# Longer contiguous runs for the r, k, v and expert-weight loads of an attention-then-experts kernel

## The chip, the cores and the metric

One core of one Trainium2 chip. The metric is device time in microseconds (us); lower is better. Times of one kernel are given as the median of its runs. Where two kernels are compared, a ratio is given too: the mean time of one kernel's fast runs over the mean of the other's fast runs from the same rounds on the same chip, with a 95% interval. It is therefore not quite the ratio of the medians. A run counts as slow when it took over 1.5% more than the fastest of its kernel.

A trace covers one execution. In it PE is TensorE's matmuls, PEld its weight loads, DVE is VectorE, ACT is ScalarE, POOL is GpSimd, SP is SyncE; a letter q after an engine's name means its sequencer, which issues DMAs. "L390" is line 390 of the kernel that the trace belongs to.

## The reference

A decayed linear attention, then a layer of experts that picks one expert for each whole sequence.

```python
B, H, S, D = 4, 8, 768, 48                 # r, k, v: [B, H, S, D] float32
state = zeros(B, H, D, D)
for t in range(S):
    kt, vt, rt = k[:, :, t], v[:, :, t], r[:, :, t]
    cur = einsum('bhd,bhe->bhde', u[None] * kt, vt)
    y[:, :, t] = einsum('bhd,bhde->bhe', rt, state + cur)
    state = w[None, :, :, None] * state + einsum('bhd,bhe->bhde', kt, vt)

x = y.transpose(0, 2, 1, 3).reshape(B, S, 384)
logits = x.mean(axis=1) @ w_gate           # [B, 8]
e = argmax(logits, axis=1)                 # one expert for a whole sequence
for b in range(B):                         # w1: [8, 384, 1024], w2: [8, 1024, 384]
    out[b] = softmax(logits)[b, e[b]] * (relu(x[b] @ w1[e[b]]) @ w2[e[b]])
```

The expert of a sequence is known only after its last row, so the weights of sequence b are loaded, and its matmuls done, while the attention of sequence b+1 runs. The last sequence's expert is a tail on its own.

## The kernel before

The attention goes in 24 chunks n of 128 rows (six per sequence). A chunk's k, r and v come by three DMAs, eight chunks ahead. A row of one head is 48 floats, so these loads move runs of 192 bytes.

```python
    AHEAD = 8
    inp = ctx.enter_context(tc.tile_pool(name="inp", bufs=AHEAD + 1))
    opool = ctx.enter_context(tc.tile_pool(name="opool", bufs=4))
    # ... (cut)
    def load(n):
        # ... (cut)
        for name, src in (("k32", k), ("r32", r), ("v32", v)):
            t = inp.tile([128, H, D], FP32, tag=name, name=f"{name}_{n}")
            nc.sync.dma_start(out=t, in_=src[b, :, s0 : s0 + C, :].transpose([1, 0, 2]))
```

GpSimd multiplies k and r by powers of the decay, TensorE transposes both (eight transposes into one PSUM tile), and ScalarE copies the eight results out in one instruction, `tw`. VectorE then forms `prod` for the bonus term, masks the scores (`gt`), adds up the chunk's output (`xn`) and masks the running state (`st`).

```python
    def prep(n):
        # ... (cut)
        nc.gpsimd.tensor_mul(kp[i][:, :, 0:D], k32, dk[:, m])
        nc.gpsimd.tensor_mul(rp[i][:, :, 0:D], r32, dr[:, m])
        vb = work.tile([128, H, D], BF16, tag="vb", name=f"vb{n}")
        nc.gpsimd.tensor_copy(vb, v32)

    def transposes(n):
        twp = pp_tw.tile([128, 2 * NP, 128], BF16, tag="tw", name=f"twp{n}")   # one PSUM buffer
        for o, src in ((NP, kp[i]), (0, rp[i])):
            for p in range(NP):
                nc.tensor.transpose(out=twp[:, o + p, :], in_=..., identity=ident)
        tw = work.tile([128, 2 * NP, 128], BF16, tag="tw", name=f"tw{n}")
        nc.scalar.copy(tw, twp)
```

The expert's weights come by two DMAs on GpSimd's queue, which also turn float32 into bf16. A partition gets three runs of `w1` and eight of `w2`. Each 128-row output tile `ob` is scaled by VectorE or ScalarE and stored by the sync queue, the same queue that issues the loads, in program order.

```python
        w1 = wpool.tile([128, NCT, F], BF16, tag="w1", name=f"w1_{b}")
        nc.gpsimd.dma_start(
            out=w1, in_=moe_w1[ds(ev, 1)].rearrange("o (ct p) f -> p (o ct) f", p=128))
        # ... w2 likewise, "o (ft p) m -> p (o ft) m" (cut)
    def mm1(b, w1, ht, ft, sb):        # hp: relu(x @ w1), 3 matmuls per tile
        #   lhsT=w1[:, ct, 128 * ft : 128 * ft + 128]
    def mm2(b, w2, ht, gw, si, half, cell):
        # ... (cut)
            ob = opool.tile([128, DM], FP32, tag="ob", name=f"ob{b}_{si}")
            # scaled by ACT for odd si, by DVE for even si
            nc.sync.dma_start(out=out[b, 128 * si : 128 * si + 128, :], in_=ob)

    for n in range(N):
        # ... (cut)
        if n + AHEAD < N:
            load(n + AHEAD)
        if n + 2 < N:
            prep(n + 2)
        if b and ci == 0:
            weights(b - 1)
        # transposes(n+1), up to five expert jobs, outputs(n), state(n), scores(n+1) ...
```

There are four buffers for `ob` and six output tiles per sequence.

## Time and profile before

| | before |
|---|---|
| time, median of 3 | 173.91 us (173.81 to 174.37) |
| span of the traced execution | 172.5 us |
| TensorE matmuls busy | 131.3 us, 76% |
| DMA packets | 85,217, of which 73,728 of 192 bytes |
| first `prod` / last expert's first `hp` / end | 13.8 / 149.7 / 172.5 us |

The table of 40 slices (each slice is 4.3 us; a digit is a share in tenths, 9 meaning 90% or more; PEclk is the granted TensorE clock):

```profile
PE   0035788768879998997007999899999979299991
PEclk9999999999999999999555899999999999969998
DMA  3989998999999989999999930059920018990042
```

Up to slice 11 TensorE is not full while the DMA engines are. From slice 12 TensorE is the limit, with one hole (slices 19 and 20, 82 to 91 us), during and after which the clock is granted by half.

The first batch has nothing but attention. The chain of waits, followed back from the end of the program, alternates there between small steps of VectorE and of TensorE (columns: start, duration, what):

```profile
21.14 0.55 DVE xn L255
21.69 0.47 DVE st L281
22.16 0.88 DVE prod L208
...
23.35 0.87 PE twp L196 x8
24.23 0.32 PE y L245 x4
24.55 0.33 PE y L250 x8
```

One round is one chunk: the next `xn` starts at 24.97, 3.84 us later.

The hole has a name in the waits (what waited, for what: us in total, times, longest):

```profile
DVE ob L390 <- DMA out_dram<-ob: 12.4, 1, 12.4
```

VectorE waited 12.4 us for the store of an earlier output tile, because all four `ob` buffers were full. The sync queue's timeline says why the store was late (start, duration, then the DMA issued):

```profile
71.78 5.45 SPq L81 DMA_DIRECT2D k<-in_k_dram  x1
77.32 4.21 SPq L81 DMA_DIRECT2D r<-in_r_dram  x1
...
86.15 0.69 SPq L81 DMA_DIRECT2D v<-in_v_dram  x1
86.93 1.27 SPq L391 DMA_DIRECT2D out_dram<-ob  x2
```

The first `ob` was begun at 71.9 us. Its store is issued at 86.93, when the queue has got through the loads that stand before it in the program.

Two groups of instructions that the change touches (after the bar: busy us in all, mean ns of one, then idle before it and for whom), and the DMA lines (packets; share of the 16 engines' time; issues with KB each and median us to landing):

```profile
L202 ACT COPY tw<-twp 128x1024 bf16<-128x1024 bf16 x24 | 24.3, 1011 | 17.9 <-PE twp L196 17.8
L365 PEld LDWEIGHTS <-w 128*128 128x128 bf16 x192 | 17.4, 103 | 15.5 <-issue 5.9
```

```profile
DMA packets 85217, 25.81 MB, mean 150 GB/s; under 512 B 76240, under 2 KB 83664, under 8 KB 85200
...
q1 hardware_dynamic: 79440, 19.29, 60.2%
q0 software_dynamic: 5760, 6.29, 22.6%
...
w<-in_moe_w_dram POOLq DMA_DIRECT2D x8, 768.0 KB, 10.9
```

q1 carries the loads and stores of the sync queue, q0 the weights.

### The profile page before, as it was taken

To read this page: it belongs to the slowest core of one execution; us is meant where nothing else is said; L and a number is where in the kernel's file an instruction comes from. 1 tells how busy PE (TensorE), PEld (TensorE's weight loads), DVE (VectorE), ACT (ScalarE), POOL (GpSimd) and SP (SyncE) were. 2 spreads that over 40 slices of the span, in tenths; PEclk is the share of its full clock that TensorE was granted. 3 is DMA by queue.
4 is the path that set the end of the run, shared out by engine and by line. 5 is a ranking of instruction groups with operands and counts; after the bars stand their busy time and mean duration, and the time that the engine had idled before them with its cause. 6 is when DMAs were issued, how large, how long until landed. Compare 5 with 4: busy or idle time off the path is not lost.

```text
span 172.5 us, 3663 instructions
## 1 busy us (share of the span) xinstructions
PE 131.3 (76%) x1392; PEld 88.9 (52%) x1392; DVE 91.5 (53%) x227; ACT 73.5 (43%) x121; POOL 87.8 (51%) x114
## 2 busy tenths in 40 slices
PE   0035788768879998997007999899999979299991
PEld 0024667657666665665004666566666454144550
DVE  3045888885785776860007567687677432022220
ACT  2929433432434674343002667334666422135221
POOL 4384788888987677667002577775661112000000
PEclk9999999999999999999555899999999999969998
DMA  3989998999999989999999930059920018990042
GB/s 88 188 153 197 187 188 166 194 179 197 177 192 198 192 164 206 174 194 185 185 243 256 256 52 6 0 91 224 245 88 0 0 49 155 226 212 0 1 174 102
DMA packets 85217, 25.81 MB, mean 150 GB/s; under 512 B 76240, under 2 KB 83664, under 8 KB 85200
## 3 DMA queue, kind: packets, MB, share of 16 engines
q1 hardware_dynamic: 79440, 19.29, 60.2%
q0 software_dynamic: 5760, 6.29, 22.6%
q8 instruction: 11, 0.18, 0.5%
q14 instruction: 6, 0.05, 0.1%
HBM read 27.15 MB, written 4.72 MB: 185 GB/s over the span
## 4 chain that ended last, share of the span: by engine, by line
PE 48%; DVE 18%; DMA 12%; issue 5%; SPq 5%; POOL 4%; ACT 4%; POOLq 0%; DVEq 0%; ACTq 0%
PE hp L365 16%; PE op L381 13%; PE twp L196 7%; SPq L81 5%; DVE prod L208 5%; DMA w<-in_moe_w_dram 5%; DVE xn L255 3%; DVE ht L374 3%; DMA ubc<-in_u_dram 3%; DMA v<-in_v_dram 2%; DVE st L281 2%; PE y L250 2%; PE y L245 2%; DMA out_dram<-ob 2%; PE xp L297 2%
## 5 line engine op out<-in xcount | busy, mean ns | idle before, releaser
L365 PE MATMUL hp<-xt,w 128*128 128x384 bf16 x192 | 42.8, 348 | 4.1 <-DMA w<-in_moe_w_dram 3.4
L236 POOL TENSOR_TENSOR vt<-vb,tcol 128x384 bf16<-128x384 bf16 x24 | 19.9, 830 | 42.6 <-DVE tcol L233 42.6
L381 PE MATMUL op<-w,ht 128*128 128x384 bf16 x192 | 35.4, 329 | 0.2 <-DVE ht L374 0.2
L202 ACT COPY tw<-twp 128x1024 bf16<-128x1024 bf16 x24 | 24.3, 1011 | 17.9 <-PE twp L196 17.8
L372 ACT ACTIVATE ht<-hp 128x384 bf16<-128x384 f32 x44 | 21.6, 492 | 20.3 <-PE hp L365 19.8
L184 POOL TENSOR_TENSOR kp<-k,dk 128x384 bf16<-128x384 f32 x24 | 23.9, 997 | 4.2 <-ACT dk L128 4.2
L365 PEld LDWEIGHTS <-w 128*128 128x128 bf16 x192 | 17.4, 103 | 15.5 <-issue 5.9
L185 POOL TENSOR_TENSOR rp<-r,dr 128x384 bf16<-128x384 f32 x24 | 24.4, 1019 | 0.0
L306 ACT COPY xt<-xp 128x384 bf16<-128x384 bf16 x24 | 11.5, 479 | 29.0 <-PE xp L297 27.7
L381 PEld LDWEIGHTS <-ht 128*128 128x128 bf16 x192 | 17.7, 99 | 10.2 <-issue 0.6
L255 DVE TENSOR_TENSOR xn<-vt,y 128x384 bf16<-128x384 bf16 x24 | 13.2, 551 | 16.2 <-PE y L250 15.2
L390 DVE TENSOR_SCALAR ob<-op,gw 128x384 f32<-128x384 f32 x12 | 7.4, 616 | 24.2 <-DMA out_dram<-ob 12.4
L374 DVE TENSOR_SCALAR ht<-hp 128x384 bf16<-128x384 f32 x20 | 11.0, 552 | 16.9 <-PE hp L365 16.6
L297 PE MATMUL xp<-ident,xn 128*128 128x128 bf16 x72 | 9.8, 257 | 10.9 <-DVE xn L255 10.9
L220 DVE TENSOR_TENSOR gt<-at,maskT 128x512 bf16<-128x512 f32 x24 | 16.4, 682 | 0.6 <-PE at L212 0.6
L234 DVE TENSOR_TENSOR gt<-at,maskT 128x512 bf16<-128x512 f32 x24 | 16.2, 677 | 0.0
L208 DVE TENSOR_TENSOR prod<-tw 128x512 bf16<-128x512 bf16 x24 | 14.2, 590 | 2.2 <-ACT tw L202 2.2
L212 PE MATMUL at<-tw 48*128 48x128 bf16 x192 | 11.6, 254 | 3.9 <-ACT tw L202 3.5
L187 POOL CAST vb<-v 128x384 bf16<-128x384 f32 x24 | 13.8, 575 | 0.0
L388 ACT ACTIVATE ob<-op,gw 128x384 f32<-128x384 f32 x12 | 7.0, 582 | 15.6 <-PE op L381 14.5
L196 PE MATMUL twp<-ident,kp 128*128 128x128 bf16 x96 | 11.7, 261 | 1.5 <-DVE U L160 1.5
L196 PE MATMUL twp<-ident,rp 128*128 128x128 bf16 x96 | 12.2, 266 | 0.0
(65 smaller groups left out, 153.3 us busy)
## 6 DMA issues: line engine op xcount, KB each, us to landing
w<-in_moe_w_dram POOLq DMA_DIRECT2D x8, 768.0 KB, 10.9
k<-in_k_dram SPq DMA_DIRECT2D x24, 192.0 KB, 4.5
r<-in_r_dram SPq DMA_DIRECT2D x24, 192.0 KB, 4.6
v<-in_v_dram SPq DMA_DIRECT2D x24, 192.0 KB, 4.6
out_dram<-ob SPq DMA_DIRECT2D x24, 192.0 KB, 3.4
wbc<-in_w_dram SPq DMA_DIRECT2D x1, 192.0 KB, 3.6
ubc<-in_u_dram SPq DMA_DIRECT2D x1, 192.0 KB, 4.4
wT<-in_w_dram SPq DMA_DIRECT2D x2, 0.8 KB, 2.8
```

The source lines that it names most:

```text
L184: nc.gpsimd.tensor_mul(kp[i][:, :, 0:D], k32, dk[:, m])
L185: nc.gpsimd.tensor_mul(rp[i][:, :, 0:D], r32, dr[:, m])
L196: nc.tensor.transpose(out=twp[:, o + p, :], in_=src[:, 2 * p : 2 * p + 2, :].rearrange("s a b -> s (a b)"), identity=ident,)
L202: nc.scalar.copy(tw, twp)
L208: nc.vector.tensor_mul(prod, tw[:, 0:NP, :], tw[:, NP : 2 * NP, :])
L220: nc.vector.tensor_mul(gt[:, 0], at[0], maskT)
L234: nc.vector.tensor_mul(gts[n][:, 1], at[1], maskT)
L236: nc.gpsimd.tensor_mul(vt, vbs[n], tcol.to_broadcast([128, H, D]))
L255: nc.vector.tensor_add(xn, vts[n].rearrange("s h d -> s (h d)"), yp[:, 0:DM])
L365: nc.tensor.matmul(out=hp[:, 0:SB], lhsT=w1[:, ct, 128 * ft : 128 * ft + 128], rhs=xts[b][:, ct, SB * sb : SB * sb + SB], start=(ct == 0), ...
L372: nc.scalar.activation(out=o, in_=hp[:, 0:SB], func=ACT.Relu)
L381: nc.tensor.matmul(out=op[:, 0:DM], lhsT=ht[:, ft, 128 * si : 128 * si + 128], rhs=w2[:, ft, :], start=(ft == 0), stop=(ft == NFT - 1),)
```

## The change

The intent is fewer, longer packets:

- **r** comes in eight groups of three chunks. Partition p of a group holds rows 3p, 3p+1, 3p+2, one run of 576 bytes per head. The columns of the transposed r then come interleaved, so the copy out of PSUM writes every third column and a chunk reads its 128 columns as one piece. A whole group must be transposed before its first chunk can start.
- **k and v** of sequences 1 to 3 come by one DMA per tensor and sequence, into a tile that keeps 16 unused columns after each row of 48.
- **Weights**: the rows of `w1` and `w2` are dealt out so that each partition's share is one run; `hp` reads its weights with a stride of eight columns to make up for it, and the output of the attention is transposed with a stride of three.
- To keep engines even, `vb` goes from GpSimd to ScalarE in the first two sequences, and `st` from VectorE to ScalarE in the first. The first three products of r are done by VectorE.
- In the program, all loads now precede the first store.

The diff, cut to its core:

```diff
-    AHEAD = 8
-    inp = ctx.enter_context(tc.tile_pool(name="inp", bufs=AHEAD + 1))
+    inp = ctx.enter_context(tc.tile_pool(name="inp", bufs=NCH))
+    binp = ctx.enter_context(tc.tile_pool(name="binp", bufs=2))
+    rinp = ctx.enter_context(tc.tile_pool(name="rinp", bufs=3))
+    rtp = ctx.enter_context(tc.tile_pool(name="rtp", bufs=3))
+    def load_batch(b):
+        for name, src in (("k32", k), ("v32", v)):
+            t = binp.tile([128, H, NCH, DP], FP32, tag=name + "b", name=f"{name}b_{b}")
+            nc.sync.dma_start(
+                out=t.rearrange("p h c d -> p (h c) d")[:, :, 0:D],
+                in_=src[b].rearrange("h (c p) d -> p (h c) d", p=128),
+            )
+    def load_r(g):
+        b, gi = divmod(g, NCH // GRP)
+        t = rinp.tile([128, H, GRP, D], FP32, tag="r32", name=f"r32_{g}")
+        nc.sync.dma_start(
+            out=t.rearrange("p h c d -> p h (c d)"),
+            in_=r[b, :, GRP * C * gi : GRP * C * (gi + 1), :].rearrange(
+                "h (p c) d -> p h (c d)", c=GRP),
+        )
     # ... (cut: issue order of the first loads, constants, the rest of prep)
-        nc.gpsimd.tensor_copy(vb, v32)
+        if n < 2 * NCH:
+            nc.scalar.copy(vb, raw.pop(("v32", n)))
+        else:
+            nc.gpsimd.tensor_copy(vb, raw.pop(("v32", n)))
+    def prep_r(j):
+        g, c = divmod(j, GRP)
+        eng = nc.vector if g == 0 else nc.gpsimd
+        eng.tensor_mul(rp[j % NR][:, :, 0:D], rraw[g][:, :, c, :], dr[:, c])
     # ... (cut: eight transposes as before, of k's chunk n and of r's chunk n + 3)
-        nc.scalar.copy(tw, twp)
+        if j < N:
+            g, c = divmod(j, GRP)
+            if c == 0:
+                rts[g] = rtp.tile([128, NP, C, GRP], BF16, tag="rt", name=f"rt{g}")
+            nc.scalar.copy(rts[g][:, :, :, c], twp[:, NP : 2 * NP, :])
+        if n >= 0:
+            kt = work.tile([128, NP, 128], BF16, tag="kt", name=f"kt{n}")
+            nc.scalar.copy(kt, twp[:, 0:NP, :])
     # ... (cut)
-            out=w1, in_=moe_w1[ds(ev, 1)].rearrange("o (ct p) f -> p (o ct) f", p=128))
+            out=w1.rearrange("p ct f -> p (ct f)"), in_=moe_w1[ds(ev, 1)].rearrange("o (p ct) f -> p (o ct f)", ct=NCT))
     # ... (cut: w2 likewise)
-                out=hp[:, 0:SB], lhsT=w1[:, ct, 128 * ft : 128 * ft + 128],
+                out=hp[:, 0:SB], lhsT=w1[:, ct, ft::NFT],
     # ... (cut)
+    for j in range(GRP):
+        prep_r(j)
     late_constants()
-    transposes(0)
+    for j in range(GRP):
+        transposes(0 if j == 0 else -1, j)
     # ... in the loop over n:
-        if n + AHEAD < N:
-            load(n + AHEAD)
+        if ci == 0 and 1 <= b and b + 1 < B:
+            load_batch(b + 1)
+        if n % GRP == 0 and n // GRP + 3 < NG:
+            load_r(n // GRP + 3)
```

## The prediction

> **What bounds the kernel now** (timeline, 40-slice table, waits):
>
> 1. 0 to 50 us: one chunk per 3.84 us (xn starts at 21.1, 25.0, 28.8, 32.7). The chain goes round DVE prod 0.88, PE bonus 0.27, eight transposes 0.87, output groups 0.65, DVE xn 0.5, DVE st 0.47. POOL (3.4 us per chunk) and the DMA engines (90% busy) run just under it.
> 2. 50 to 138 us: TensorE, 0.9 busy, 4.5 to 5 us per chunk, with one hole from 80.6 to 91.6 us. The waits name it: DVE's ob waits 12.4 us for the output store. All four ob buffers are full because the first store issues at 86.9 us: the sync queue is in order and still pushing loads (0.9 to 5.5 us per issue instead of 0.4[...]). The granted clock is 0.5 from 82.8 to 96.4 us (six hp in 1.94 us, later 1.15).
> 3. The tail: 8.0 us of waiting for the last w1, then matmuls.
>
> Loads are bound by packets: 73,728 of 192 B, median 15 ns each per engine, about 1.0 us per 1,024; 1,536 B take 66 ns. The Trainium skill ("DMA: Bandwidth & Descriptors", Specifications) asks for 512 B or more for line rate; the trace agrees (12.8 against 23 B/ns).
>
> **What the change does**
>
> - r: 24 loads of 192 B runs become 8 of 576 B. Estimated from those two sizes at 29 ns a packet: 24 us of DMA become 15. k and v keep 49,152 packets of 192 B, in fewer DMAs: 48 us, unchanged.
> - Weights: 1,408 packets per expert (9.7 us) become a few hundred long ones; I expect 8.5 to 9 us, 0.7 off the tail.
> - All loads now precede the stores and depend only on buffers, so they run ahead. DMA work up to the last load sums to 84 us, against 101; the first store should issue near 80 us, when ob4 is nearly wanted. The stall shrinks from 10.6 us to 0 to 3, and the half clock goes too: the skill ("TensorE: Matmul & The Clock Gate", Part 1) puts it after an idle window of about 3.4 us.
> - First batch: st goes to ACT, vb leaves POOL: 0.47 us off the chain, 3.35 per chunk.
> - Added before the first score: three rp products on DVE (0.6 each), three transposes with copies one after another in one PSUM buffer, ubc behind a larger r load: first prod at 18 instead of 13.8 us. tw (1.01) becomes two ACT copies of about 0.59. The first batched v load, 6,144 packets, may land 0 to 4 us late for chunk 6.
> - Strided weight loads for hp should hide behind 164 ns matmuls.
>
> **Sum:** start +4.5, first-batch chain -2.5, late v +2, stall -9, clock -2.5, tail -0.7, fewer conflicts -0.7: 165 us, range 159 to 171. Faster by over 2%: 0.82; within 2%: 0.14; slower: 0.04.
>
> **Right if** ob's wait for the store falls below 4 us, the half clock after 80 us vanishes, packets drop below 69,000, the first xn starts near 22 us, chunks of batch 0 are 3.35 us apart. **A step is wrong if** r packets take well over 29 ns, or hp exceeds 164 ns each.
>
> **What would make it wrong:** large k and v DMAs block the sync queue as long as before, so the stall stays (171); chunk 6 waits longer; strided weight loads or ACT copies slow the TensorE stage; or the start costs less (160).

## More of the kernel before

The four groups of experiments ran on three chips, at different times, and the kernel before took 173.9 to 176.3 us in them (medians), so kernels of different groups are compared by their ratios to the kernel before.

The clock's row prints 9 also where the trace has no record, and before 55.5 us it has none. What the clock was there shows in the spacing of the transposes: one every 107 ns up to 55 us, as in the recorded half clock at 95 us, and one every 56 ns from there on. So the first 55 us ran at half the clock.

## The result, and the profile after

| | before | after |
|---|---|---|
| time, median | 173.86 us of 4 (173.80 to 174.37) | 185.62 us of 4 (183.73 to 186.89) |
| ratio of fast runs | | 1.0588 (95%: 1.053 to 1.0647) |
| span of the traced execution | 172.5 us | 185.1 us |
| TensorE matmuls busy | 131.3 us, 76% | 135.1 us, 73% |
| DMA packets | 85,217 | 35,585 |

The change made the kernel slower by about 6%. Two of the four runs after count as slow; the ratio leaves them out. The trace after spans 185.1 us (the record gives 182.8 for the profiled run). That is at the long end of the four timed executions, whose spans were 181.8 to 185.0 us, and would count as slow by the same rule, so the differences between the two traces add up to 12.6 us where the ratio says about 10. The steps on which the argument rests come back in fast runs: the late start in a_now and a_ob6, the first hole in a_now, the second in b_w.

The 40 slices after (4.6 us each):

```profile
PE   0013558865678799899809999899399989299990
PEclk9999999999999999999995899999969999969999
DMA  3889999989999999999962000099410016980042
```

TensorE starts later, and there are now two holes: slice 20 (93 to 97 us) is the old one, and slice 28 (130 to 134 us) is new. After each the clock falls.

The waits after:

```profile
DVE ob L444 <- DMA out_dram<-ob: 8.8, 2, 7.2
...
DVE prod L255 <- ACT rt L242: 6.0, 1, 6.0
...
ACT ob L442 <- DMA out_dram<-ob: 3.3, 1, 3.3
...
ACT vb L218 <- DMA v32b<-in_v_dram: 2.9, 1, 2.9
```

The first line is the wait that should have gone: 7.2 us of it remain from the first hole, and 1.6 with the 3.3 of ScalarE's line are the second. The other two lines are the new start and the first batched v.

The sync queue's timeline, and the three DMAs in the chain of waits that answer to it (start, duration):

```profile
23.30 7.34 SPq L90 DMA_DIRECT2D v32b<-in_v_dram  x1
...
66.05 9.19 SPq L90 DMA_DIRECT2D v32b<-in_v_dram  x1
75.34 7.27 SPq L100 DMA_DIRECT2D r<-in_r_dram  x1
83.54 7.25 SPq L445 DMA_DIRECT2D out_dram<-ob  x3
```

```profile
23.30 17.99 DMA v32b<-in_v_dram
...
83.54 12.52 DMA out_dram<-ob
...
122.24 10.96 DMA out_dram<-ob
```

The first store is indeed asked for earlier, at 83.54 instead of 86.93, but takes 12.5 us to land instead of 3.4, because the loads asked for just before it are still in the engines (counted below, under the step that failed). A store at 122.24, which has no counterpart in the old chain, takes 11 us.

The start, in ScalarE's timeline (the bracket says how long the engine was idle before, and what released it):

```profile
15.83 1.01 ACT L242 COPY rt<-twp 128x512 bf16<-128x512 bf16 x1 [5.21 <-PE twp L233]
...
17.93 1.01 ACT L242 COPY rt<-twp-1_1_238 128x512 bf16<-128x512 bf16 x1 [0.67 <-PE twp-1_1_238 L233]
19.62 1.01 ACT L242 COPY rt<-twp-1_2_244 128x512 bf16<-128x512 bf16 x1 [0.67 <-PE twp-1_2_244 L233]
```

The three copies of the first r group go one after another through the single PSUM buffer, each of the first two followed by the next four transposes. The first `prod` starts at 20.66, against 13.76.

The groups and DMA lines that answer to those of before:

```profile
L419 PEld LDWEIGHTS <-w 128*128 128x128 bf16 x192 | 25.3, 151 | 15.0 <-issue 7.6
...
L242 ACT COPY rt<-twp 128x512 bf16<-128x512 bf16 x22 | 22.5, 1024 | 11.6 <-PE twp L233 11.2
...
L245 ACT COPY kt<-twp 128x512 bf16<-128x512 bf16 x24 | 15.0, 623 | 0.2 <-PE twp L233 0.2
```

```profile
DMA packets 35585, 25.81 MB, mean 139 GB/s; under 512 B 13808, under 2 KB 34544, under 8 KB 35568
...
q1 hardware_dynamic: 34416, 19.28, 49.6%
q0 software_dynamic: 1152, 6.29, 18.1%
...
w<-in_moe_w_dram POOLq DMA_DIRECT2D x8, 768.0 KB, 11.5
```

So the DMA engines do have less to do, and that is not where the time is. Note `rt`: copying half of the columns (512) takes 1.02 us, as long as all 1,024 took before, and `kt` comes on top.

**Where the 12.6 us lie.** Comparing the start of `prod` of the same chunk in both traces gives the lag of the kernel after, and its steps:

| up to | lag, us | step |
|---|---|---|
| chunk 0 (13.8, 20.7) | 6.9 | start +6.9 |
| chunk 4 (29.9, 36.9) | 7.0 | first batch's chain +0.1 |
| chunk 5 (33.6, 43.2) | 9.6 | v late +2.6 |
| chunk 14 (76.3, 87.3) | 11.0 | +1.4 |
| chunk 15 (91.9, 97.7) | 5.8 | first hole shorter, −5.2 |
| chunk 21 (123.6, 130.5) | 6.9 | +1.1 |
| chunk 22 (128.5, 139.9) | 11.4 | second hole +4.5 |
| last expert's first `hp` (149.7, 161.3) | 11.6 | +0.2 |
| end (172.5, 185.1) | 12.6 | +1.0 |

### The profile page after: what moved, and what is told of

It is laid out like the page before. It is cut to its first block, busy times and chain, and to the rows that moved or that the text cites. A ratio compares the mean times of both kernels' runs of the same rounds, so it can differ in the third digit from the quotient of the medians.

```text
span 185.1 us, 3577 instructions
## 1 busy us (share of the span) xinstructions
PE 135.1 (73%) x1392; PEld 98.0 (53%) x1392; DVE 93.8 (51%) x229; ACT 91.0 (49%) x165; POOL 75.4 (41%) x99
## 2 busy tenths in 40 slices
DMA packets 35585, 25.81 MB, mean 139 GB/s; under 512 B 13808, under 2 KB 34544, under 8 KB 35568
## 3 DMA queue, kind: packets, MB, share of 16 engines
q0 software_dynamic: 1152, 6.29, 18.1%
## 4 chain that ended last, share of the span: by engine, by line
PE 37%; DMA 33%; SPq 12%; DVE 7%; ACT 5%; issue 4%; POOLq 1%; ACTq 0%; DVEq 0%
PE hp L419 17%; DMA out_dram<-ob 13%; DMA w<-in_moe_w_dram 10%; DMA v32b<-in_v_dram 10%; PE op L435 8%; SPq L83 7%; PE twp L233 2%; PE lgp L375 2%; PE xp L351 2%; PE at L259 2%; ACT rt L242 2%; SPq L120 1%; DVE ht L428 1%; ACT ht L426 1%; SPq L100 1%
## 5 line engine op out<-in xcount | busy, mean ns | idle before, releaser
L419 PE MATMUL hp<-xt,w 128*128 128x384 bf16 x192 | 45.3, 364 | 7.5 <-DMA w<-in_moe_w_dram 4.0
L419 PEld LDWEIGHTS <-w 128*128 128x128 bf16 x192 | 25.3, 151 | 15.0 <-issue 7.6
L242 ACT COPY rt<-twp 128x512 bf16<-128x512 bf16 x22 | 22.5, 1024 | 11.6 <-PE twp L233 11.2
L226 POOL TENSOR_TENSOR rp<-r,dr 128x384 bf16<-128x384 f32 x21 | 20.9, 998 | 5.3 <-DMA r<-in_r_dram 5.3
L360 ACT COPY xt<-xp 128x384 bf16<-128x384 bf16 x24 | 11.5, 478 | 19.8 <-PE xp L351 19.0
L428 DVE TENSOR_SCALAR ht<-hp 128x384 bf16<-128x384 f32 x20 | 11.1, 553 | 18.1 <-PE hp L419 17.8
L259 PE MATMUL at<-rt,kt 48*128 48x128 bf16 x192 | 11.7, 255 | 11.5 <-ACT kt L245 10.3
L255 DVE TENSOR_TENSOR prod<-kt,rt 128x512 bf16<-128x512 bf16 x24 | 14.1, 587 | 9.8 <-ACT rt L242 6.0
L215 POOL TENSOR_TENSOR kp<-k32b,dk 128x384 bf16<-128x384 f32 x18 | 18.0, 999 | 0.0
L259 PEld LDWEIGHTS <-kt 48*128 48x128 bf16 x192 | 6.7, 108 | 17.8 <-ACT kt L245 15.2
L245 ACT COPY kt<-twp 128x512 bf16<-128x512 bf16 x24 | 15.0, 623 | 0.2 <-PE twp L233 0.2
L233 PE MATMUL twp<-ident,rp 128*128 128x128 bf16 x88 | 11.0, 265 | 2.9 <-DVE U L193 2.9
## 6 DMA issues: line engine op xcount, KB each, us to landing
w<-in_moe_w_dram POOLq DMA_DIRECT2D x8, 768.0 KB, 11.5
```

What stands on the lines that cost most here:

```text
L215: nc.gpsimd.tensor_mul(kp[n % NR][:, :, 0:D], raw.pop(("k32", n)), dk[:, m])
L226: eng.tensor_mul(rp[j % NR][:, :, 0:D], rraw[g][:, :, c, :], dr[:, c])
L233: nc.tensor.transpose(out=twp[:, o + p, :], in_=src[:, 2 * p : 2 * p + 2, :].rearrange("s a b -> s (a b)"), identity=ident,)
L242: nc.scalar.copy(rts[g][:, :, :, c], twp[:, NP : 2 * NP, :])
L245: nc.scalar.copy(kt, twp[:, 0:NP, :])
L259: nc.tensor.matmul(out=at[a][:, p, :], lhsT=kt[64 * a : 64 * a + D, p, :], rhs=rtn[64 * a : 64 * a + D, p, :], start=True, stop=True,)
```

## The experiments

Names: `b_` kernels are built from the kernel before, `a_` from the one after. `ob6` has six output buffers, `w` the new weight layout, `eng` the moves of `vb` and `st` to ScalarE, `nor` r loaded per chunk again, `nokv` k and v loaded per chunk again. All gave correct results, but for the two marked.

### Group 1: weights and stores

**b_w: the new weight layout alone.** The rival to "the weights are harmless" is that their long packets hold up the stores.

```diff
-    nc.sync.dma_start(out=wg, in_=moe_w_gate.rearrange("(ct p) e -> p ct e", p=128))
+    nc.sync.dma_start(out=wg, in_=moe_w_gate.rearrange("(p ct) e -> p ct e", p=128))
-                out=xp[:, ct, :], in_=xn[:, 128 * ct : 128 * ct + 128], identity=ident
+                out=xp[:, ct, :], in_=xn[:, ct::NCT], identity=ident
     # ... (cut: the second use of xn, and w2, likewise)
-            out=w1, in_=moe_w1[ds(ev, 1)].rearrange("o (ct p) f -> p (o ct) f", p=128))
+            out=w1.rearrange("p ct f -> p (ct f)"), in_=moe_w1[ds(ev, 1)].rearrange("o (p ct) f -> p (o ct f)", ct=NCT))
-                out=hp[:, 0:SB], lhsT=w1[:, ct, 128 * ft : 128 * ft + 128],
+                out=hp[:, 0:SB], lhsT=w1[:, ct, ft::NFT],
```

> The kernel before with only the weights' part of the change: w1, w2, the gate's weights in one run per partition, and the strided reads that go with it. Theory (long weight packets take the DMA engines' turns from the output stores): weight packets become 6,144 B of about 473 ns each, and a second wait of ob for a store appears while the third expert's weights load (near 112 to 125 us), total 176 to 180 us. Rival (strided weight reads slow TensorE): no such wait, but the hp matmuls are spaced well over 164 ns in the tail, total 176 to 180 as well. Rival (weights only get faster): 172 to 174.

Measured: 178.05 us, ratio 1.0236 (1.0143 to 1.033). The second hole is there without any other part of the change: `prod` of chunks 21 and 22 lie 9.3 us apart, against 4.9 before. Its waits:

```profile
DVE ob L390 <- DMA out_dram<-ob: 13.4, 2, 12.2
...
ACT ob L388 <- DMA out_dram<-ob: 3.4, 1, 3.4
```

The line of ScalarE is new, and alike to the one of the kernel after.

**a_now: the change without the weight layout.** The same lines undone in the kernel after.

```diff
-            out=w1.rearrange("p ct f -> p (ct f)"), in_=moe_w1[ds(ev, 1)].rearrange("o (p ct) f -> p (o ct f)", ct=NCT))
+            out=w1, in_=moe_w1[ds(ev, 1)].rearrange("o (ct p) f -> p (o ct) f", p=128))
     # ... (cut: the other lines)
```

> The changed kernel with the old weight layout (three and eight runs per partition, natural order). Theory: the second stall, near 122 to 133 us in the changed kernel, goes, and the time falls by 4 to 6 us to about 180. Rival (strided weight reads): it falls too, but the stall stays. If neither matters: 185.

Measured: 182.26 us, ratio 1.0457 (1.0375 to 1.0539). The second hole is gone (chunks 21 and 22: 4.8 us apart; ScalarE's `ob` no longer waits for a store), the first is not (`ob` on VectorE waits 6.8 us). The time fell by less than the 4 to 6 us expected. In the traces the hole comes with the layout and goes with it; in time the layout costs 2.4% by b_w, and undoing it gives back 1.3 points, the latter across two groups of runs whose intervals (1.053 to 1.0647 and 1.0375 to 1.0539) overlap a little. The strided reads are there in b_w_cut too, where the hole is gone, so they are not its cause.

How long packets hold up a store can be counted from the packets of the trace. These are the packets begun in one microsecond, while weights and a store share the engines (my count; bytes x number, mean ns):

```
before, 116 to 117 us:  weights 2,048 B x 78, 172 ns    store 1,536 B x 64, 78 ns
after,  124 to 125 us:  weights 6,144 B x 31, 473 ns    store 1,536 B x 32, 78 ns
```

(Weight packets are counted by the trace in bytes of bf16, as they arrive.) In the kernel after, store and weight packets alternate about one to one. A store has 128 packets, 8 for each engine; an estimate from these numbers is 8 x (473 + 78) ns = 4.4 us for one store, and the store of 122.24 us stands behind the one of 119.75. From 123 to 130 us the stores get through at 21 to 43 packets per us; when the weights end, at 130, the rate jumps to 187. The Trainium skill ("DMA: Bandwidth & Descriptors", Queues, rings and completion order) says that each DMA engine takes turns between queue rows packet by packet; the count agrees, 31 to 32 here, and 162 to 165 in a_now at 92 us (768-byte packets of weights against 576-byte packets of r).

**b_ob6 and a_ob6: six output buffers instead of four,** in the kernel before and in the one after. If both holes are waits for a free `ob`, both must go.

```diff
-    opool = ctx.enter_context(tc.tile_pool(name="opool", bufs=4))
+    opool = ctx.enter_context(tc.tile_pool(name="opool", bufs=6))
```

> The kernel before with six instead of four buffers for ob, so that no output tile of a batch waits for a store of the same batch. Theory (the hole at 80 to 91 us comes from a store stuck behind loads): the hole and the half clock after it go, 161 to 164 us. Rival (the loads themselves are late there, the ob wait only hides it): 170 to 174.

Measured: 161.71 us, ratio 0.9276 (0.9208 to 0.9344). From the page of this run, in 40 slices of 4.0 us:

```profile
PE   0016588986878999899999997999999794699990
PEclk9999999999999999999999999999999999789999
```

The hole and the half clock at 80 to 96 us are gone. The first store is issued at 87.67 us, no earlier than before; nothing has to wait for it any more. One changed digit in the kernel before is worth 12 to 13 us, more than the 9 that the whole change was to gain.

> The changed kernel with six ob buffers. Theory: both stalls go (first about 5.5 us over the normal chunk spacing, second about 4.5): 174 to 177 us, that is still 11 to 14 us over the kernel before with six buffers, because the late start (7 us) and the late v load (3 us) stay. Rival (stalls are due to data arriving late): 182 to 186.

Measured: 172.72 us, ratio 0.9923 (0.9852 to 0.9995). Both holes are gone here too (chunks 14 and 15: 4.6 us apart, 21 and 22: 4.8), and the time is a little under the 174 to 177 us expected. With the stores out of the way, the change still costs 11 us: `prod` of chunk 0 lags that of b_ob6 by 6.6 us, of chunk 5 by 8.8, of chunk 23 by 10.7. So the stores explain the missing gain, and something in the r, k and v loads explains a loss. The next groups part it.

### Group 2: which of r, k and v costs

All kernels from here on have six output buffers.

**a_ob6_nor: r per chunk again,** k and v batched.

```diff
-    for o, src, on in ((NP, rp[j % NR], j < N), (0, kp[n % NR], n >= 0)):
+    for o, src in ((NP, kp[i]), (0, rp[i])):
     # ... eight transposes, one copy tw as before; r32 loaded per chunk, 8 ahead, as before
```

> Changed kernel, six ob buffers, r loaded per chunk in natural order again (one copy of both transposes, no rows of r in front of the first score, but k and v of later batches still in one DMA each, weights new, st and vb on ACT). Theory (the batched v load, landing at 41.4 us, sets when chunk 6 can go on, and hides the late start): the first prod returns to about 14 us, but the wait for v grows from 2.9 to about 10 us because 20 small loads now stand ahead of it; total 172 to 175, as with six buffers alone (172.7). Rival (the late start adds to everything after it): 165 to 167.

Measured: 177.56 us, ratio 1.0174 (1.0078 to 1.027), slower than with r grouped. That is above the 172 to 175 us expected. The start is indeed back (first `prod` at 13.9 us), and all of it is lost again at the v of chunk 6, which is in the first batched load: its copy `vb` stands ahead of chunk 5's copies in ScalarE's order, so `prod` of chunk 5 starts at 44.2 us, later than in a_ob6 (42.6). After it the first expert's weights land at 67.4 instead of 62.8 us, and the trace ends 4.8 us later than that of a_ob6. The wait:

```profile
ACT vb L209 <- DMA v32b<-in_v_dram: 13.0, 1, 13.0
```

**a_ob6_nokv: k and v per chunk again,** r grouped.

```diff
+    AHEAD = 8
-    load_batch(1)
-        if ci == 0 and 1 <= b and b + 1 < B:
-            load_batch(b + 1)
+        if n + AHEAD < N:
+            load(n + AHEAD)
     # ... (cut: pools, order of the first loads)
```

> Changed kernel, six ob buffers, k and v loaded per chunk for all batches, eight chunks ahead, r grouped as in the change. Theory: the wait for v goes, the late start (first prod at 20.6) stays and now shows in full: prod of chunk 5 at about 40.5 instead of 42.6 us, total 169.5 to 171. Rival (the batched loads are the main cost, over their slower bytes too): 163 to 166.

Measured: 170.03 us, ratio 0.9741 (0.9657 to 0.9826). The late v is gone (chunk 5 starts at 40.4 instead of 42.6 us), the late start stays.

**a_ob6_flat: the r copies side by side instead of every third column.** This gives a wrong result (relative error 1.28): rows keep r's permuted order. The number and size of all instructions stay.

```diff
-                rts[g] = rtp.tile([128, NP, C, GRP], BF16, tag="rt", name=f"rt{g}")
-            nc.scalar.copy(rts[g][:, :, :, c], twp[:, NP : 2 * NP, :])
+                rts[g] = rtp.tile([128, NP, GRP, C], BF16, tag="rt", name=f"rt{g}")
+            nc.scalar.copy(rts[g][:, :, c, :], twp[:, NP : 2 * NP, :])
     # ... (cut: a chunk reads [:, :, m, :]; the decay columns of the natural order)
```

> Changed kernel, six ob buffers, wrong result on purpose: the copies of transposed r write 128 columns side by side instead of every third, and the decay columns are those of the natural order; sizes and loads stay. Theory: the copy falls from 1.02 to about 0.6 us, the first prod comes 1.2 to 1.6 us earlier, chunks 1 to 4 are 3.3 to 3.5 us apart instead of 3.75, but chunk 6 then waits the longer for v, so the total falls by under 1 us (172). Rival (the copies' time is on the path to the end): 168.5 to 170.5.

Measured: 173.14 us, ratio 0.9927 (0.9839 to 1.0015), no different from a_ob6. Yet the copies did get faster, as the group's line shows, and the wait for v took the gain back:

```profile
L242 ACT COPY rt<-twp 128x512 bf16<-128x512 bf16 x22 | 12.9, 584 | 11.9 <-PE twp L233 11.5
```

```profile
ACT vb L218 <- DMA v32b<-in_v_dram: 4.8, 1, 4.8
```

The copies went from 1,024 to 584 ns and the first `prod` from 20.6 to 16.6 us, but chunk 5 starts at 42.1 instead of 42.6. What was gained before the arrival of the batched v did not count. That makes the batch a wall: earlier work is hidden behind it.

The edit does one thing more than it was meant to. Side by side, a chunk's columns of r come from one copy alone, so the first `prod` no longer waits for the third copy (what released it in the trace is `kt`, where it is the third `rt` in a_ob6). Most of the 4.0 us at the first `prod` is that; the `prod` of chunk 1 starts only 1.8 us earlier (23.9 instead of 25.7).

**b_ob6_eng: the kernel before with six buffers and the moves of `vb` and `st`.**

```diff
-        nc.gpsimd.tensor_copy(vb, v32)
+        if n < 2 * NCH:
+            nc.scalar.copy(vb, v32)
+        else:
+            nc.gpsimd.tensor_copy(vb, v32)
     # ... and st on ScalarE for the first sequence, into tiles zeroed once
```

> Kernel before, six ob buffers, plus the change's moves of work: vb on ACT for the first two batches, st on ACT in the first. Theory (the chain prod, transposes, outputs, xn, st sets the 3.84 us): chunks 1 to 5 are 3.35 to 3.5 us apart and the total is 159 to 160.5, against 161.7. Rival (the chunk is held by POOL and tcol, or by the loads): spacing above 3.7 and 161 to 163.

Measured: 160.03 us, ratio 0.9189 (0.9094 to 0.9284). The first batch's chunks lie 3.2 us apart on average (`prod` of chunks 1 to 5: 19.2, 22.1, 25.7, 28.8, 32.1), against 3.8 in b_ob6. So the engine moves do what the prediction said of them, but in the kernel before, not together with the grouped r (3.7 in a_ob6_nokv).

### Group 3: the copies without the wall, the whole without r's and k's layout, and the gap

**a_ob6_nokv_flat: side-by-side copies, k and v per chunk** (wrong, relative error 1.28). The edit is that of a_ob6_flat on a_ob6_nokv.

> Changed kernel, six ob buffers, k and v per chunk, and the side-by-side copies of r (wrong result on purpose). The same edit of the copies that changed nothing (172.7 to 173.1) while the batched v load held chunk 6. Theory (the v landing was a wall, and without it the late start and the slower chunks of the first batch count in full): first prod at 16.6 instead of 20.4 us, chunks 3.35 to 3.5 us apart, total 163.5 to 166. Rival (the first batch's pace is absorbed later anyway): 169 to 170.

Measured: 167.34 us, ratio 0.9502 (0.9419 to 0.9586). That lies between the expectation and its rival. Without the wall the same edit takes the ratio from 0.9741 to 0.9502, about 4 us, but across two groups of runs; the medians differ by 2.7 us and the traces by 2.1 at the end (chunk 5 starts 2.0 us earlier, chunk 23 2.7). The first `prod` comes at 16.9 us, against 20.4, but chunk 1 only 1.3 us earlier, about the three shorter copies. So the strided copy was a cost of 2 us or somewhat more, hidden by the wall in a_ob6_flat; the dependency that goes with it (above) was not parted from it.

**b_ob6_eng_w: b_ob6_eng with the new weight layout.**

> Kernel before, six ob buffers, vb and st moved to ACT, plus the new weight layout. Theory (the layout costs only through the stores): LDWEIGHTS of hp near 150 ns again but hidden, total 159.3 to 160.7 against 160.0. Rival (strided weight reads or the layout itself cost): 162 to 165.

Measured: 161.0 us, ratio 0.9136 (0.9043 to 0.9228); one of its four runs (164.85) counts as slow. With enough output buffers the weight layout costs nothing that these rounds can show, though the median is just above the range expected (159.3 to 160.7). This kernel is also the fourth corner of a square, all with six buffers, the new weight layout and the engine moves:

| ratio to before | k, v per chunk | k, v in batches |
|---|---|---|
| r per chunk | 0.9136 (b_ob6_eng_w) | 1.0174 (a_ob6_nor) |
| r in groups of three | 0.9741 (a_ob6_nokv) | 0.9923 (a_ob6) |

Each part alone costs: r's grouping 6 points, k and v's batching 10. Together they cost 8, less than the sum and less than batching alone: the wall at chunk 6 hides r's late start, and the grouped r loads take less engine time. The corners come from three groups of runs, so a difference of one point between them is not certain; these are larger.

Of r's share the strided copies are the smaller part. In the traces b_ob6_eng_w ends at 157.6 us and a_ob6_nokv, which groups r, at 167.9; a_ob6_nokv_flat, grouped but not strided, still ends at 165.8. Much of that is there at chunk 1 (19.2, 25.5 and 24.2 us), in the start, where a whole group is loaded, multiplied and transposed first.

**a_ob6_nopad: the batched tile without its gap** of 16 columns after each row. Its rival is that a gap in SBUF costs nothing.

```diff
-            t = binp.tile([128, H, NCH, DP], FP32, tag=name + "b", name=f"{name}b_{b}")
+            t = binp.tile([128, H, NCH, D], FP32, tag=name + "b", name=f"{name}b_{b}")
-                out=t.rearrange("p h c d -> p (h c) d")[:, :, 0:D],
+                out=t.rearrange("p h c d -> p (h c) d"),
     # ... (cut: the slices of the tile)
```

> Changed kernel, six ob buffers, the batched k and v tiles without the gap of 16 columns per row, so each partition is written as one piece. If the gap makes the batched loads slow (164 GB/s against about 195 for the per-chunk loads), v lands at 38 to 39.5 instead of 41.4 us and the total is 170 to 171.5. If the long walk over the source does, nothing changes: 172 to 173.5.

Measured: 170.94 us, ratio 0.9699 (0.9625 to 0.9772), about 2 points better than a_ob6 across two groups of runs; the traces end 1.7 us apart, and the first batched v lands at 39.0 instead of 40.7 us. A batched load moves in packets of 768 bytes, four rows of 192 (my count from the packets; the rate is the median over the microseconds in which nothing else moved):

```
                        packet     median   k, v loads
a_ob6 (gap)             768 B      86 ns    about 164 GB/s
a_ob6_nopad (no gap)    768 B      71 ns    about 187 GB/s
before, per chunk       192 B      15 ns    about 190 GB/s
```

The batched loads, which were to be at least as fast, are slower than the 192-byte loads that they replace, and the gap is the reason: without it they are level. They are still not faster, though the packets are a quarter as many. Why is not shown; the rows read from HBM are 192 bytes long in both cases.

**b_w_cut: the new weight layout, each weight DMA cut in two halves of the columns,** so that packets are 1,024 and 384 bytes. This was to mend b_w.

```diff
-            out=w1, in_=moe_w1[ds(ev, 1)].rearrange("o (ct p) f -> p (o ct) f", p=128))
+        for x in range(2):
+            cs = slice(F // 2 * x, F // 2 * (x + 1))
+            nc.gpsimd.dma_start(out=w1[:, :, cs], in_=s1[:, :, cs])
     # ... (cut: w2 likewise; the new layout as in b_w)
```

> Kernel before with the new weight layout, but each weight load cut in two halves by columns, so that packets are at most 1,024 B again while rows, layout and strided reads stay. Theory (packets of 6,144 B take the stores' turns): the second wait of ob, at 120 to 131 us, goes; total 173 to 175.5. Rival (layout or strided reads): 177 to 179 as with whole rows.

Measured: 181.03 us, ratio 1.0277 (1.0199 to 1.0355): a miss on the time. The second hole did go (chunks 21 and 22: 4.9 us apart), with the layout and the strided reads kept, so short weight packets do let stores through. But the weights now took 47.6 us of the 16 engines' time (sum of packet times over 16), where they took 38.9 before and 33.4 in the kernel after; the remaining loads came later, the first store was issued at 90.9 instead of 86.9 us, and `ob` waited 15.0 us for it. Shorter packets helped the one hole and widened the other; that the longer weight loads are what delayed the others is the likely cause, not tested on its own.

### Group 4: the best version, and one batched load that is asked for in time

Open was whether the batch is bad only because it lands late, or also where it is asked for early.

**b_kv3: b_ob6_eng_w with only the last sequence's k and v batched,** asked for eight chunks ahead.

```diff
+        if n + AHEAD == N - NCH:
+            load_batch(B - 1)
-            load(n + AHEAD)
+            load(n + AHEAD, ("k32", "r32", "v32") if n + AHEAD < N - NCH else ("r32",))
```

> Kernel before, six ob buffers, vb and st moved, new weight layout, and only the last batch's k and v in one DMA each, asked for eight chunks before its first chunk; all else per chunk. Theory (batched loads hurt because the whole batch must land before its first chunk can start, and in the first batch there is no lead): with this lead no vb waits for v, total within 1.5 us of the same kernel without it (159 to 162). Rival (the large DMAs themselves cost, wherever they stand): 164 or more.

Measured, over five rounds: 167.04 us, ratio 0.9508 (0.9453 to 0.9564); it was a miss, because the batch's own v is no longer waited for but the kernel is slower all the same. The waits show one for r, and the sync queue's timeline the reason:

```profile
POOL rp L203 <- DMA r<-in_r_dram: 4.0, 1, 4.0
```

```profile
77.24 16.83 SPq L84 DMA_DIRECT2D r<-in_r_dram  x3
```

Three small r loads took 16.8 us to issue, because they stood behind the two large ones. They landed from 95.3 us on, after the batched v (94.5). In these runs a batch was late for its own reader or made others late. This batch kept the gap of a_ob6; without it, it was not tried.

**best_eng and best_eng_w: b_ob6_eng and b_ob6_eng_w again,** beside it, over five rounds.

> The best combination so far once more, to choose between it and the one with the new weight layout on one chip: ratio to before 0.91 to 0.925.

> The same with the new weight layout. Theory (the layout costs nothing once stores have buffers): ratio within 0.006 of the one without it. Rival (strided reads or long packets still cost): at least 0.01 higher.

Measured: best_eng 161.1 us, ratio 0.9174 (0.9129 to 0.9219); best_eng_w 162.24 us, ratio 0.9156 (0.9095 to 0.9218), two of six runs slow. The intervals overlap, so the weight layout shows neither a gain nor a loss. In best_eng_w a v load of chunk 11 lands behind the long packets of the first expert's weights (`vb` waits 4.1 us once), which the trace of best_eng does not show (that of b_kv3, which has the layout too, does: 4.0 us), so it is not free of effects.

The best version is the kernel before with six output buffers and the moves of `vb` and `st`: 160 to 161 us, 8% faster than before and about 13% faster than after. The output buffers alone give 7 of the 8 points.

## Why the prediction was wrong, point by point

| term of the sum | predicted | measured between the traces | shown by |
|---|---|---|---|
| start | +4.5 | +6.9 | timeline; a_ob6_flat and a_ob6_nokv_flat |
| first batch's chain | −2.5 | +0.1 | b_ob6_eng, a_ob6_nokv_flat |
| late v | +2 | +2.6 | a_ob6_nokv |
| first store's stall and its half clock | −9 and −2.5 | −5.2 together | b_ob6, a_ob6 |
| tail | −0.7 | +0.2 to the last expert's first `hp`, +1.0 after it | last w1 landed in 8.0, then 8.2 us; last store in 1.9, then 2.9 us |
| fewer conflicts | −0.7 | not seen | |
| weights against stores | none | +4.5 | b_w, a_now |

The remaining +2.5 lies in small steps of chunks 5 to 14 and 15 to 21, which no run took apart. The +1.0 at the end is the last store alone, which lands 1.9 us after its issue in all other traces but that of a_now (2.8), so it does not belong to the change.

**The step that failed** is "All loads now precede the stores and depend only on buffers, so they run ahead. ... The stall shrinks from 10.6 us to 0 to 3, and the half clock goes too". The first store was issued earlier, at 83.5 us, close to the "near 80" of the prediction. But it was taken for done when issued. It landed 12.5 us later, since the last batched v and r loads and the weights of the second expert were still in the engines. From 85 to 91 us the trace counts 31 to 34 weight packets begun per us, and 1 to 43 of the r load that stands before the store in its queue; when the weights end, r's packets go to 227 and then 493 per us, and the first packets of the store come at 92 us. With the old weight layout it is no better (a_now: 12.1 us to landing), so here it is the amount in front of the store and not the length of the weight packets. So the buffer came free 5.7 us later than before (96.06 against 90.32 us), and the stall got shorter only because the program reached it 11 us later. The prediction's own warning, that large loads block the queue as long as before and the stall stays, came close, but put 171 us to it.

**A whole term was missing.** The prediction put down the long weight packets as a gain of 0.7 us on the tail and did not ask what shares the engines with them. Their share of the engines' time did fall (22.6% to 18.1%), their landing did not get shorter (10.9 to 11.5 us), and the stores of the same window had to wait behind packets of 473 ns. b_w shows the term alone: +2.4%.

**Start and chain were mis-sized, in part by one wrong duration.** "tw (1.01) becomes two ACT copies of about 0.59" holds for `kt` (0.62) and for side-by-side copies (0.58), but the copies to every third column took 1.02. Three of them stand one after another at the start (about 1.3 us more than assumed, 3 x (1.01 - 0.59), of the 2.4 by which the start was longer than predicted), and in each chunk of the first batch `kt` follows `rt`, so that `prod` waits for it: 3.7 us per chunk (`prod` of chunks 1 to 4) instead of 3.35. Side by side it was still 3.5 (a_ob6_nokv_flat, chunks 1 to 5), so the grouping slows the chain without the stride too; by which of its steps is open. The rest of the start is `ubc`, behind a larger r load (`uw` at 10.63 instead of 8.86 us), and the three products of r that VectorE does ahead of U's copies (13.35 instead of 10.16). The prediction had named both.

**The late v had the right size and the wrong nature.** It was taken as 2 us to add. It was a point in time, some 40 us, behind which earlier gains were lost: it landed at 41.29 us here, and where the start was mended (a_ob6_nor) chunk 6 waited 13.0 us for it.

**Right:** packets fell far below 69,000; r's packets took 29 ns at the median (33.7 on average), so r's loads went from 28.9 to 17.3 us of the 16 engines' time, a fall of about the size estimated (24 to 15); and the strided weight loads, 151 instead of 103 ns, stay hidden: the tail's first-layer matmuls took 11.35 us after and 11.30 before. k and v's packets became 768 bytes, not 192 as predicted, and their engine time stayed all the same (57.8 before, 59.3 after), as foretold. None of these was on the critical path.

**The half clock** followed the holes: before from 82.8 to 96.4 us, after from 96.7 to 103.5 and from 134.2 to 137.7, and neither is there in b_ob6. Each of the three traces has another right after the wait for the last weights (151.0 to 154.5 before, 161.6 to 165.0 after, 137.9 to 141.4 in b_ob6). The Trainium skill ("TensorE: Matmul & The Clock Gate", Part 1) puts the half clock after an idle window of about 3.4 us. That is the right size, but less than a whole window was enough here: in the kernel before the clock fell 1.8 us after the last matmul (81.0 us), and the second hole of the kernel after was only 2.9 us long (131.1 to 133.9).

**What stays open.** The first batch runs at half clock without such a hole, in the kernel before up to 55.5 us (shown above) and in the best version too (best_eng: recorded from 26.4 to 29.9 and from 33.3 to 53.8 us); this was not taken apart. Stores on a queue of their own, a weight packet between 2,048 and 6,144 bytes, or r grouped without strided copies and a serial start were not tried in a correct kernel.

## What to carry to other kernels

Before making transfers longer, look in the waits for what the program really waits for: here it was a free output buffer, and two more buffers gave 7% where the change that halved the packets lost 6%. A transfer has an end as well as an issue: in these runs one large load turned many small deadlines into a single one at its end and delayed what stood behind it in the same queue, and longer packets made the other queue's packets wait for their turn. If a new layout needs a strided write or more copies in a serial start, measure that one copy first, because it may be paid on the critical path while the saved DMA time is not.

## What the Trainium skill lacked or had wrong

- "DMA: Bandwidth & Descriptors", Rules for kernel authors, advises coalescing many small transfers into one large one. It warns of transfers under 64 KB, and these were above that. Here 192-KB loads of 192-byte rows ran at 190 GB/s, and a batch of six of them in one DMA at 164 GB/s into rows with a gap in SBUF, 187 without; and its 18 us to landing became a wall. The page gives no cost of a gap on the SBUF side (packet median 86 against 71 ns), and does not speak of the single late landing.
- The same page, Queues, rings and completion order, has the packet-wise turns right (31 against 32 packets in one us), but draws no consequence: weight packets of 473 ns stretched the landing of a store to 11 us (after), and the layout that made them cost 2.4% (b_w).
- The same page, SWDGE vs HWDGE vs iDMA, calls packets of 4,096 bytes or less preferable. The traces record 6,144-byte packets for the casting weight loads, at 473 ns, moving 13.0 bytes per ns against 11.9 for 2,048 bytes (172 ns) and 9.8 for 768 bytes (78 ns): the length past 2,048 bought little, which agrees with the page; it gives no cost for longer ones.
- "Advanced Engine Details and Errata", Memory Cachelines, says that a 16-byte line needs at least two hits to absorb the access latency. ScalarE's copy writing bf16 at a stride of 6 bytes, which hits such a line two or three times, still took 1,024 ns against 584 side by side (a_ob6_flat). No page gives a cost for ScalarE's strided writes.
- "TensorE: Matmul & The Clock Gate", Weight-path perf modes, names packed and strided weight reads side by side and gives no cost for the stride. At a stride of 16 bytes (8 columns of bf16) a weight load took 151 ns against 103; it was hidden here behind the matmuls.
